# Three small transfers of the softmax denominators moved from SyncE's queue to GpSimd's, with GpSimd held to program order

## The chip, the cores and the metric

The kernel runs on one core of one Trainium2 chip. The metric is the device time of one execution in microseconds (us). The core has five engines that run side by side, each through its own list of instructions in order: TensorE (PE in the profile; its weight loads are PEld), VectorE (DVE), ScalarE (ACT), GpSimd (POOL) and SyncE (SP). SP computes nothing here and issues most of the transfers (DMAs); POOL issues a few of its own. An instruction that waits for a semaphore holds up everything behind it on its engine, and that goes for an issued DMA too.

## What is computed

A layer over 2048 tokens of width 1024: a layer norm, softmax attention with 32 heads of width 32, a gate that routes the best 8 tokens through a SwiGLU network, and their product added to the input.

```python
xn = layernorm(x)
q, k, v = split(xn @ wqkv)                       # 32 heads of 32
o = softmax(q @ k.T / sqrt(32)) @ v              # per head
s = o @ wo
r = xn @ w_r;  idx = top 8 of r over the tokens
y = (silu(xn[idx] @ w_gate) * (xn[idx] @ w_up)) @ w_down * sigmoid(r[idx])
out = x + s * silu(xn with y added at rows idx)
```

## The kernel before

Attention runs over 8 groups g of four heads, 4 blocks qb of 512 queries in each, and 16 key tiles kt in each block: 32 blocks of 16 units. They are numbered here block 0 to 31, and a unit is written (block, kt). In a unit PE makes the scores `sc` of four heads in two halves, ACT takes their exponentials into a tile `pt` of [128, 4 x 512] float32 (L390, two instructions), PE multiplies them with the values into `oa` (L404), and DVE adds `pt` to the block's running sum (`add`, L397, 15 in a block; the first `pt` of a block is itself the sum). PE fills the rest of a unit with the projections of the next groups, in blocks 20 to 28 also with the routed feed-forward network (`ffn` L618, `py` L649). There are five `pt` buffers; one holds the running sum of the block, and for the first units of a block another still holds that of the block before. So an exponential may have to wait for the add of the unit four (early in a block three) before it.

The sum over the 128 partitions of a finished running sum gives the softmax denominators. For blocks 0 to 27 this is done by transfers, called a fold here, numbered like its block. After the end of block b, in units of block b+1:

- unit 1, `fold`: SP stores the sum to DRAM (`a_d`, L438, 1 MB). POOL then issues the ladder, three accumulating DMAs within `a_d` (L440), of 64, 32 and 16 rows added onto as many others, each waiting for the one before.
- unit 9, `fold_load`: the 16 rows left are read back into `dr16` (L446) as 128 x 16 pieces of 16 floats, 64 bytes each.
- unit 12, `fold_rows` and `reciprocals`: DVE sums the 16 rows (L450), takes the reciprocals (L456) and adds to two running checks (L458, L459). One unit later the reciprocals are stored (`r_d`, L462, 128 pieces of 64 bytes), and after that spread over partitions (`rb`, L467, 128 rows of 2 KB).
- units 1 and 2 of block b+2: DVE multiplies the block's output with `rb` (`normalise`, L473), and it is split and stored.

Blocks 28 to 31 (the last group, g == L) get their denominators by matmul (`sums`) and then use the same `reciprocals`.

The order of PE, DVE, ACT and SP is the order in which the program's text issues the work (`manual_schedule`), unit by unit. SP issues in that one order the loads of weights (`wf` L606 and `wd` L611 of the feed-forward network, into three buffers, each waiting for PE to be done with the tile three before; `wo` L691), the stores and loads of q, k and v, and, of each fold, L438, L446, L462 and L467. POOL's order is left to the scheduler of the framework, which issues what is ready first by its own estimate. POOL has few other tasks: two `iota` (L536, L562), a gather of routed rows (L576), a maximum over partitions of weight magnitudes `am` (L1094, `partition_all_reduce`, whose result DVE reads at L1097), and in the last blocks a memset and a gather `up` per tile (L701, L702). Instructions that load another program into POOL stand ahead of the first `iota` and ahead of L1094; order listings show them as `ISA`.

Of the kernel before, what the change touches and what calls it, by code (L numbers as in the profile page):

```python
# [54 lines left out]
@with_exitstack  # L55
def kernel(ctx, tc, x, wqkv, wo, w_r, w_gate, w_up, w_down, out,
                                      general=True, force_general=False):
    nc = tc.nc
    x = x.rearrange("b s d -> (b s) d")
    out = out.rearrange("b s d -> (b s) d")  # L60

    dram = ctx.enter_context(tc.tile_pool(name="dram", bufs=1, space=bass.MemoryType.DRAM))
    keep = ctx.enter_context(tc.tile_pool(name="keep", bufs=1))
    y_d = dram.tile([C, D], F32, name="y_d")
    slot_d = dram.tile([P, NT], I32, name="slot_d")
    ok_i = keep.tile([P, 1], I32, name="ok_i")

    with ExitStack() as st:
        _fast(st, tc, x, wqkv, wo, w_r, w_gate, w_up, w_down, out, dram, y_d, slot_d, ok_i,
              force_general)  # L70

    if general:
        ok = nc.values_load(ok_i[0:1, 0:1], min_val=0, max_val=P)
        with tc.If(ok < P):
            with ExitStack() as st:
                _general(st, tc, x, wqkv, wo, out, dram, y_d, slot_d)
# [28 lines left out]
def _fast(ctx, tc, x, wqkv, wo, w_r, w_gate, w_up, w_down, out, dram, y_d, slot_d, ok_i,  # L105
          force_general):
    nc = tc.nc
# [155 lines left out]
    L = NG - 1  # L263
# [179 lines left out]
    def fold_load(g, qb):  # L443
        a_d = DN[g, qb]
        dr = DN[g, qb] = sb.tile([P, 16, 16], F32, name="dr16", tag="rb", bufs=1)
        nc.sync.dma_start(dr, a_d[0:16].rearrange("r (p q) -> p r q", q=16))  # L446

    def fold_rows(g, qb):
        dr = small.tile([P, 2, 16], F32, name="dr", tag="dr")
        nc.vector.tensor_reduce(dr[:, 0], DN[g, qb].rearrange("p r q -> p q r"), axis=AX.X, op=ALU.add)  # L450
        DN[g, qb] = dr
        return reciprocals(g, qb)

    def reciprocals(g, qb):
        dr = DN[g, qb]
        nc.vector.reciprocal(dr[:, 1], dr[:, 0])  # L456
        r_d = dram.tile([4, 512], F32, name="r_d", tag="r_d", bufs=2)
        nc.vector.tensor_add(den_f, den_f, dr[:, 0])  # L458
        nc.vector.tensor_add(rec_f, rec_f, dr[:, 1])  # L459

        def store():
            nc.sync.dma_start(r_d.rearrange("j (b q) -> (j b) q", q=16), dr[:, 1])  # L462
            return 1, spread

        def spread():
            rb = DN[g, qb] = sb.tile([P, 512], F32, name="rb", tag="rb", bufs=1)
            nc.sync.dma_start(rb, bass.AP(tensor=r_d.tensor, offset=r_d.offset, ap=[[512, 4], [0, 32], [1, 512]]))  # L467

        return 1, store

# [405 lines left out]
    for b in range(NG * NB):  # L876
        g, qb = divmod(b, NB)
        for k, f in (((1, sums), (5, reciprocals), (9, normalise), (10, split_o)) if g == L else
                     ((1, fold), (9, fold_load), (12, fold_rows), (17, normalise), (18, split_o))):
            if b < NG * NB - 1:  # L880
                at((b + 1) * NT + k, f, g, qb)
# [4 lines left out]
    def go(f):  # L886
# [6 lines left out]

    order = ExitStack()
    order.enter_context(tc.manual_schedule(
        engines={mybir.EngineType.PE, mybir.EngineType.DVE, mybir.EngineType.Activation, mybir.EngineType.SP}))


    todo, held, steps = [], [], []
# [98 lines left out]
    for t in range(2, NT + 1):  # L998
# [22 lines left out]
        b, tt = divmod(done, 4)  # L1021
# [27 lines left out]
    for i, u in enumerate(units):  # L1049
        g, qb, kt = u  # L1050
# [27 lines left out]
    for n, f in enumerate(rest_of):  # L1078
        clock[0], ready = len(units) + n, due.pop(len(units) + n, [])
        go(f)  # L1080
        for h in ready + (sides[:1] if n % 2 else []):
            go(h)
        if n % 2:
            sides = sides[1:]
        for k, h in ((2, sums), (12, reciprocals), (24, normalise), (26, split_o)):
            if n == k:
                go(lambda: h(L, NB - 1))
# [172 lines left out]
```

## Time and profile before

| | |
|---|---|
| median of 3 runs | 1640.17 us (1639.65 to 1643.1) |
| profiled execution | 1639.18 us, of which 1637.4 us lie between its first and last instruction |
| busy share of that span | PE 99%, DVE 88%, ACT 72%, POOL 7% |
| granted TensorE clock | 0.998 |
| DMA | 260.87 MB, mean 159 GB/s |

The busy share of PE is an upper mark, since matmuls overlap and their ends are modelled. The span of the profiled execution is what the stretches below add up to; 1.8 us lie outside it.

### The profile page before, as it was taken

Reading aid. Unit: us, or ns where it says so; the run is one execution under the profiler, and the core shown is the slowest. Engines: PE = TensorE matmul, PEld = TensorE weight load, DVE = VectorE, ACT = ScalarE, POOL = GpSimd, SP = SyncE. Lnnn points to the kernel's source line nnn. Section 1 sums busy time; section 2 is a strip of 40 time slices with the busy share of each in tenths; the row PEclk is TensorE's granted clock in tenths of the full one; section 3 lists DMA queues with packets and bytes.
Section 4 is the critical chain, followed back from the end, with each engine's and each line's share of the span. In section 5 each row is a group of like instructions: output and inputs, shape, how many; then the busy total and the mean of one; then the engine's idle time right before and its main releaser. Section 6 shows DMA issues by size and latency. Waiting matters only on the chain.

```text
span 1637.4 us, 59551 instructions
## 1 busy us (share of the span) xinstructions
PE 1615.4 (99%) x27209; PEld 1008.9 (62%) x27209; DVE 1439.4 (88%) x1150; ACT 1178.1 (72%) x1314; POOL 114.8 (7%) x125
## 2 busy tenths in 40 slices
PE   8899999999999999999999999999999999999998
PEld 7646565788875557788655555567454543455566
DVE  8868999999999999999999998888999989787862
ACT  5677777777787787787877877777777777665520
POOL 0000000000000000000000000000000101121010
PEclk9999999999999999999999999999999999999999
DMA  8935555445643454556645577677877877534442
GB/s 286 197 91 131 132 152 139 123 132 131 171 115 83 112 138 116 129 144 163 156 128 145 138 206 198 175 209 213 226 204 211 239 209 206 157 118 139 167 152 94
DMA packets 236093, 260.87 MB, mean 159 GB/s; under 512 B 102994, under 2 KB 183170, under 8 KB 232250
## 3 DMA queue, kind: packets, MB, share of 16 engines
q1 hardware_dynamic: 225866, 231.12, 47.3%
q0 software_dynamic: 9968, 25.87, 10.6%
q8 instruction: 215, 3.52, 0.9%
q14 instruction: 44, 0.36, 0.1%
HBM read 185.25 MB, written 99.43 MB: 174 GB/s over the span
## 4 chain that ended last, share of the span: by engine, by line
PE 83%; DVE 7%; DMA 5%; issue 3%; ACT 1%; SPq 1%; POOL 0%; DVEq 0%; ACTq 0%; POOLq 0%
PE sc L259 23%; PE oa L404 23%; PE proj L259 16%; PE wop L259 10%; PE vp L259 7%; DVE pt L397 3%; DMA a_d<-a_d 2%; PE ffn L618 1%; DMA a_d<-pt 1%; DVE stt L164 1%; PE vp L306 1%; PE py L649 1%; DVE xh L214 1%; ACT pt L390 1%; DMA z<-in_A_x_dram 0%
## 5 line engine op out<-in xcount | busy, mean ns | idle before, releaser
L390 ACT ACTIVATE pt<-sc 128x1024 f32<-128x1024 f32 x1024 | 997.5, 1024 | 343.6 <-PE sc L259 246.5
L397 DVE TENSOR_TENSOR pt<-pt 128x2048 f32<-128x2048 f32 x480 | 1096.1, 2287 | 43.7 <-ACT pt L390 22.1
L259 PE MATMUL sc<-qs,ks 96*32 96x512 f16 x8192 | 658.5, 380 | 3.4 <-ACT pt L390 3.2
L404 PE MATMUL oa<-pt,v 128*32 128x512 f32 x4096 | 551.9, 593 | 0.0
L259 PE MATMUL proj<-xt,w 128*32 128x512 f16 x5664 | 443.5, 379 | 0.0
L259 PEld LDWEIGHTS <-ks 96*32 96x32 f16 x8192 | 293.0, 97 | 119.9 <-issue 19.5
L259 PEld LDWEIGHTS <-w 128*32 128x32 f16 x5664 | 212.5, 96 | 187.0 <-issue 124.6
L404 PEld LDWEIGHTS oa<-pt,v 128*32 128x32 f32 x4096 | 166.0, 110 | 64.4 <-ACT o L415 0.5
L259 PEld LDWEIGHTS <-xt 128*32 128x32 f16 x4608 | 150.4, 96 | 83.8 <-issue 66.6
L259 PE MATMUL vp<-w,xt 128*32 128x256 f16 x4608 | 184.7, 272 | 0.0
L259 PE MATMUL wop<-wo,ot 128*32 128x512 f16 (+1 forms) x3168 | 173.1, 372 | 0.0
L440 POOL DMA_DIRECT2D a_d<-a_d x84 | 67.8, 808 | 1241.2 <-DMA a_d<-pt 939.8
L259 PEld LDWEIGHTS <-ot 128*32 128x32 f16 x3168 | 108.3, 97 | 73.0 <-issue 21.6
L357 DVE SCALAR_TENSOR_TENSOR hl<-proj,hl 128x512 f16<-128x512 f32 x61 | 41.9, 687 | 50.9 <-ACT hl L356 50.8
L763 DVE SCALAR_TENSOR_TENSOR z<-wop,z 128x512 f32<-128x512 f32 (+1 forms) x33 | 22.1, 674 | 59.0 <-PE wop L259 58.8
L306 PE MATMUL vp<-w,xt 128*128 128x256 f16 x384 | 44.1, 273 | 5.1 <-DMA xt<-xh 5.1
L306 PEld LDWEIGHTS <-xt 128*128 128x128 f16 x384 | 36.9, 98 | 11.5 <-DMA xt<-xh 6.6
L618 PEld LDWEIGHTS ffn<-wf,xst 128*32 128x32 f32 x512 | 19.1, 109 | 37.1 <-issue 34.3
L356 ACT ACTIVATE hl<-proj 128x512 f16<-128x512 f32 x61 | 36.4, 596 | 5.1 <-PE proj L259 4.3
L618 PE MATMUL ffn<-wf,xst 128*32 128x224 f32 x512 | 37.3, 352 | 1.1 <-DMA wf<-in_B_w_up_dram 1.1
L249 DVE SCALAR_TENSOR_TENSOR w<-wraw,w 128x1024 f16<-128x1024 f32 x24 | 29.2, 1217 | 3.4 <-ACT w L244 3.3
L252 DVE TENSOR_REDUCE am<-wraw 128x1 f32<-128x1024 f32 x24 | 28.8, 1210 | 0.0
(139 smaller groups left out, 598.2 us busy)
## 6 DMA issues: line engine op xcount, KB each, us to landing
a_d<-pt SPq DMA_DIRECT2D x28, 1024.0 KB
st<-hl SPq DMA_DIRECT2D x64, 256.0 KB
a_d<-a_d POOLq DMA_DIRECT2D x28, 512.0 KB, 6.6
wf<-in_B_w_gate_dram SPq DMA_DIRECT2D x32, 448.0 KB
wf<-in_B_w_up_dram SPq DMA_DIRECT2D x32, 448.0 KB
wd<-in_B_w_down_dram SPq DMA_DIRECT2D x32, 448.0 KB
wraw<-in_A_wqkv_dram SPq DMA_DIRECT2D x24, 512.0 KB
ks<-st SPq DMA_DIRECT2D x96, 128.0 KB
```

What stands on the lines that cost most here:

```text
L249: nc.vector.scalar_tensor_tensor(hl[:, 1], WR[c, g], WS, hl[:, 0], op0=ALU.mult, op1=ALU.subtract)
L252: nc.vector.tensor_reduce(am[:, c * NG + g:c * NG + g + 1], WR.pop((c, g)).rearrange("p k f -> p (k f)"), axis=AX.X, op=ALU.max, apply_abs ...
L259: nc.tensor.matmul(out[c], w[:, c], x, **flags)
L306: nc.tensor.matmul(box["ps"][:, tt], xt[:, xi, k, t % 4 * P:(t % 4 + 1) * P], w[:, :, wi, k, :], start=(n == 0), stop=(n == 23))
L356: nc.scalar.activation(hl[:, 0], ps, AF.Copy, scale=KQ)
L357: nc.vector.scalar_tensor_tensor(hl[:, 1], ps, KQ, hl[:, 0], op0=ALU.mult, op1=ALU.subtract)
L390: nc.scalar.activation(PT[u][:, 2 * hf:2 * hf + 2], ps, AF.Exp, bias=0.0, scale=ESC)
L397: nc.vector.tensor_add(ACC[g, qb], ACC[g, qb], PT[u])
L404: nc.tensor.matmul(OA[g, qb][32 * j:32 * j + 32, :], VT[g, kt // 2][:, kt % 2, 32 * j:32 * j + 32], PT[u][:, j, :], start=(kt == 0), stop= ...
L440: nc.gpsimd.dma_start(a_d[0:n], a_d[n:2 * n], accum_op=ALU.add, max_dma_last_dim=4096)
L618: nc.tensor.matmul(box[i][32 * j:32 * j + 32, :], RT["xst"][:, k, :], wt[:, j * FQ:(j + 1) * FQ], start=(k == 0), stop=(k == KT - 1))
L763: nc.vector.scalar_tensor_tensor(z, box["ps"][:, c0:c0 + width], WOD, z, op0=ALU.mult, op1=ALU.mult)
```

## The change

For blocks 0 to 27 the read of the folded rows (L446), the store of the reciprocals (L462, now L463) and their spread (L467, now L468) are issued by POOL instead of SP. POOL joins the engines that keep program order. For the last group the store and the spread stay on SP. From L456 on, lines after the change are one higher, and from L894 on two higher.

```diff
     def fold_load(g, qb):
         a_d = DN[g, qb]
         dr = DN[g, qb] = sb.tile([P, 16, 16], F32, name="dr16", tag="rb", bufs=1)
-        nc.sync.dma_start(dr, a_d[0:16].rearrange("r (p q) -> p r q", q=16))
+        nc.gpsimd.dma_start(dr, a_d[0:16].rearrange("r (p q) -> p r q", q=16))
...
     def reciprocals(g, qb):
         dr = DN[g, qb]
+        queue = nc.sync if g == L else nc.gpsimd
...
         def store():
-            nc.sync.dma_start(r_d.rearrange("j (b q) -> (j b) q", q=16), dr[:, 1])
+            queue.dma_start(r_d.rearrange("j (b q) -> (j b) q", q=16), dr[:, 1])
             return 1, spread
 
         def spread():
             rb = DN[g, qb] = sb.tile([P, 512], F32, name="rb", tag="rb", bufs=1)
-            nc.sync.dma_start(rb, bass.AP(tensor=r_d.tensor, offset=r_d.offset, ap=[[512, 4], [0, 32], [1, 512]]))
+            queue.dma_start(rb, bass.AP(tensor=r_d.tensor, offset=r_d.offset, ap=[[512, 4], [0, 32], [1, 512]]))
...
     order.enter_context(tc.manual_schedule(
-        engines={mybir.EngineType.PE, mybir.EngineType.DVE, mybir.EngineType.Activation, mybir.EngineType.SP}))
+        engines={mybir.EngineType.PE, mybir.EngineType.DVE, mybir.EngineType.Activation, mybir.EngineType.SP,
+                 mybir.EngineType.Pool}))
```

**SP around fold 27 (block 28).** SP's order before, where the read of the folded rows stands between the loads of `wd`, `wo` and the store and spread of the reciprocals:

```order
L372 DMA qs<-st 32x4x512 x3
L611 DMA wd<-in_B_w_down_dram 112x1024
L446 DMA dr_25496<-a_d 128x16x16
L691 DMA wo_25528<-wo_d 128x1024
L611 DMA wd<-in_B_w_down_dram 112x1024
L691 DMA wo_25528<-wo_d 128x1024
L611 DMA wd<-in_B_w_down_dram 112x1024
L691 DMA wo_25528<-wo_d 128x1024
L462 DMA r_d<-dr 128x16
L691 DMA wo_25528<-wo_d 128x1024
L467 DMA rb<-r_d 128x1x512
```

The same place after the change:

```order
L372 DMA qs<-st 32x4x512 x3
L612 DMA wd<-in_B_w_down_dram 112x1024
L692 DMA wo_25528<-wo_d 128x1024
L612 DMA wd<-in_B_w_down_dram 112x1024
L692 DMA wo_25528<-wo_d 128x1024
L612 DMA wd<-in_B_w_down_dram 112x1024
L692 DMA wo_25528<-wo_d 128x1024 x3
L660 DMA y_d<-y 8x256 x4
```

The three transfers of the fold are gone from SP, and the loads close up. It is the same at every fold.

**POOL around fold 25 (block 26).** POOL's order before: only the ladders, and the maximum `am` between two of them:

```order
L440 DMA a_d<-a_d 128x1024
L440 DMA a_d<-a_d 64x1024
L440 DMA a_d<-a_d 32x1024
L1094 ISA
L1094 ISA am<-am 128x32
L440 DMA a_d<-a_d 128x1024
```

After the change:

```order
L440 DMA a_d<-a_d 64x1024
L440 DMA a_d<-a_d 32x1024
L446 DMA dr_24056<-a_d 128x16x16
L1096 ISA
L1096 ISA am<-am 128x32
L463 DMA r_d<-dr 128x16
L468 DMA rb<-r_d 128x1x512
L440 DMA a_d<-a_d 128x1024
```

The load of POOL's other program and the maximum (now L1096) stand behind the read of fold 25 and ahead of its store and spread. At fold 8 the `iota` L537 with such a load ahead of it stands between the ladder and the read in the same way; before, that load stood at the start of the program, ahead of the other `iota`.

**DVE at fold 25 (block 26).** DVE's order after the change, with the semaphores that each row waits for (DMASW are transfers issued by POOL, Pool is POOL itself):

```order
L397 TENSOR_TENSOR pt<-pt 128x2048 [waits DVE_49,Activation_49]
L450 TENSOR_REDUCE dr<-dr_24056 128x16 [waits DMASW7_49,DMASW2_49]
L1099 TENSOR_REDUCE fl<-am 128x1 [waits Pool_49]
L1100 TENSOR_REDUCE fl<-am 128x1
L457 RECIPROCAL dr<-dr 128x16 [waits DVE_49]
L459 TENSOR_TENSOR den_f<-den_f,dr 128x16
```

Nothing moved on DVE: before, the same rows (L1097 for L1099) stand in the same order. L450 waited for a transfer issued by SP there, and now for POOL's.

## Rows read from the trace of the kernel before

**Rows 1.** The page, parts 1 and 4: busy time of each engine, and the chain of work that ended last by engine.

```profile
PE 1615.4 (99%) x27209; PEld 1008.9 (62%) x27209; DVE 1439.4 (88%) x1150; ACT 1178.1 (72%) x1314; POOL 114.8 (7%) x125
...
PE 83%; DVE 7%; DMA 5%; issue 3%; ACT 1%; SPq 1%; POOL 0%; DVEq 0%; ACTq 0%; POOLq 0%
```

**Rows 2.** Busy time by stretch of 100 us: start and end, length, then PE, PEld, DVE, ACT and POOL busy us (instructions), granted clock, DMA share, GB/s.

```profile
300.00:400.00 100.00, 100.00 (x1803) 80.30 (x1797) 93.66 (x67) 78.22 (x88) 4.81 (x6) 1.00 0.45 121
1300.00:1400.00 100.00, 94.83 (x1402) 41.62 (x1395) 88.68 (x61) 76.00 (x84) 11.35 (x11) 0.98 0.78 212
```

**Rows 3.** Who waited for whom, all engines: us in total, times, longest us.

```profile
PE py L649 <- DMA wd<-in_B_w_down_dram: 1.8, 1, 1.8
...
DVE o L473 <- DMA rb<-r_d: 2.9, 4, 1.0
...
PE ffn L618 <- DMA wf<-in_B_w_up_dram: 1.1, 1, 1.1
```

**Rows 4.** The same for SP's own queue.

```profile
SPq L462 <- DVE rec_f L459: 192.9, 31, 9.7
...
SPq L446 <- DMA a_d<-a_d: 77.7, 24, 6.4
```

**Rows 5.** SP in order of time: start us, us, engine, line, operation, out<-in, count. From folds 0, 25, 26 and 27.

```profile
158.45 0.38 SPq L446 DMA_DIRECT2D dr<-a_d  x1
...
1266.78 0.38 SPq L446 DMA_DIRECT2D dr<-a_d  x1
...
1307.95 0.55 SPq L352 DMA_DIRECT2D v<-v_d  x1
1313.40 0.38 SPq L446 DMA_DIRECT2D dr<-a_d  x1
1313.88 1.50 SPq L606 DMA_DIRECT2D wf<-in_B_w_up_dram  x2
...
1349.17 0.37 SPq L611 DMA_DIRECT2D wd<-in_B_w_down_dram  x1
1355.31 0.38 SPq L446 DMA_DIRECT2D dr<-a_d  x1
...
1357.46 0.43 SPq L611 DMA_DIRECT2D wd<-in_B_w_down_dram  x1
```

**Rows 6.** PE in order of time at folds 26 and 27; in brackets the idle time before a row and what ended it.

```profile
1306.35 0.56 PE L618 MATMUL ffn<-wf,xst 128*32 128x224 f32 x8
...
1318.23 0.59 PE L618 MATMUL ffn<-wf,xst 128*32 128x224 f32 x8 [1.06 <-DMA wf<-in_B_w_up_dram]
...
1351.15 0.62 PE L649 MATMUL py<-wd,ht 112*32 112x256 f32 x8
...
1361.94 1.08 PE L649 MATMUL py<-wd,ht 112*32 112x256 f32 x8 [1.84 <-DMA wd<-in_B_w_down_dram]
```

**Rows 7.** POOL in order of time: the first `iota`, the last ladder step of fold 8, the first and the last step of a ladder (fold 24), and the end of fold 25's ladder with the maximum behind it.

```profile
9.52 0.14 POOL L562 IOTA ti<- 128x16 int32 x1 [9.06 <-issue]
...
503.76 0.78 POOL L440 DMA_DIRECT2D a_d<-a_d  x1 [5.52 <-DMA st<-hl]
...
1207.41 0.83 POOL L440 DMA_DIRECT2D a_d<-a_d  x1 [32.03 <-DMA a_d<-pt]
...
1220.47 0.78 POOL L440 DMA_DIRECT2D a_d<-a_d  x1 [5.12 <-DMA a_d<-a_d]
...
1261.69 0.78 POOL L440 DMA_DIRECT2D a_d<-a_d  x1 [4.40 <-DMA a_d<-a_d]
1270.52 2.38 POOL L1094 PARTITION_ALL_REDUCE am<-am  x1 [8.05 <-DVE am L252]
```

**Rows 8.** The page, part 6: POOL's ladder steps of 128 KB, count, size and median us from issue to landing.

```profile
a_d<-a_d POOLq DMA_DIRECT2D x28, 128.0 KB, 3.5
```

**Rows 9.** Groups of instructions by line on POOL: operation, count, busy us, mean ns of one, idle time before. The gather of 128 rows.

```profile
L702 POOL DMA_INDIRECT up<-y_d,slot_i x16 | 26.6, 1664 | 10.7 <-DMA y_d<-y 6.5 <-POOL up L701 3.5 <-issue 0.6
```

**Rows 10.** DVE in order of time: the first fold's L450, the first use of the `iota` of L536, block 26 around fold 25, and L450 of folds 26 and 27.

```profile
172.27 0.62 DVE L450 TENSOR_REDUCE dr<-dr 128x16 f32<-128x256 f32 x1
...
513.86 0.28 DVE L538 TENSOR_TENSOR hot<-hot,pf 1x128 f32<-1x128 f32 x1
...
1275.03 0.59 DVE L450 TENSOR_REDUCE dr<-dr 128x16 f32<-128x256 f32 x1
1275.54 0.17 DVE L1097 TENSOR_REDUCE fl<-am 128x1 f32<-128x32 f32 x1
...
1276.09 2.28 DVE L397 TENSOR_TENSOR pt<-pt 128x2048 f32<-128x2048 f32 x1
...
1281.29 2.28 DVE L397 TENSOR_TENSOR pt<-pt 128x2048 f32<-128x2048 f32 x1
...
1316.42 0.63 DVE L450 TENSOR_REDUCE dr<-dr 128x16 f32<-128x256 f32 x1
...
1359.52 0.59 DVE L450 TENSOR_REDUCE dr<-dr 128x16 f32<-128x256 f32 x1
```

**Rows 11.** ACT in order of time: the exponentials of units (27, 1) and (27, 3), each unit two instructions, and the first row after a late load in block 29.

```profile
1280.04 1.04 ACT L390 ACTIVATE pt<-sc 128x1024 f32<-128x1024 f32 x1
...
1283.79 1.94 ACT L390 ACTIVATE pt<-sc 128x1024 f32<-128x1024 f32 x2 [0.39 <-PE sc L259]
...
1397.65 1.24 ACT L711 ACTIVATE z<-z,nmr,rstd_r 128x1024 f32<-128x1024 f32 x1 [2.09 <-DMA z<-in_A_x_dram]
```

## The prediction

> **What bounds the kernel now.** The page first: PE is busy for 99% of the span and makes up 83% of the chain that ended last [rows 1]. By stretches, 300 to 400 us shows PE busy for all 100 us and DVE for 93.66: PE sets the pace, and DVE follows with little to spare. From 1300 to 1400 us PE is busy for only 94.83 us [rows 2]. So nearly everywhere this change has nothing to win, and much to lose if it holds up DVE; a gain can come only from the 5 us that PE is idle in blocks 27 to 29. The waits name who causes them: PE waits 1.1 us for a `wf` tile and 1.8 us for a `wd` tile [rows 3].
>
> SP's queue shows why those tiles were late. SP stands at L446 for ladders for 77.7 us in all and at L462 for DVE's reciprocals for 192.9 us [rows 4]. Mostly nobody misses what queues behind. Twice somebody does. At fold 26 SP is done with L352 at 1308.5 us and held at L446 until 1313.40; behind it stands the `wf` load that PE wants at 1317.2 [rows 5, 6]. At fold 27 it is held from 1349.5 to 1355.31, and the `wd` load behind it is issued at 1357.46 for a use that PE reaches at 1360.1 [rows 5, 6].
>
> **What the change removes.** Both holds. The `wf` load needs the buffer of the use at 1306.35, free at 1306.9; without L446 it can go at about 1308.6, 5 us sooner, and PE's idle 1.06 us vanishes. The `wd` load needs the use of 1351.15 to be over, at 1351.8, so it can go at about 1352, also 5 us sooner, and 1.84 us vanish [rows 5, 6]. Sum: -2.9 us. I take it whole, with nothing as the other bound: if the loads are slow for want of bandwidth (DMA share 0.78 there [rows 2]), less is won.
>
> The Trainium skill (DMA: Bandwidth & Descriptors, section "Issuing engines are not separate DMA queues") says that spreading transfers over engines only saves the time an engine's sequencer takes to initiate them, since all run on the same 16 DMA engines. By that rule alone the gain is nothing, since the 0.38 us of an issue is not what held PE, and the sum below would be +3.0 us, 1643.2. The rows show something else to win, the hold of an in-order queue, so I keep the -2.9.
>
> **What it adds on POOL: the price of a transfer.** No plain read or spread by POOL is in the trace; the ladder is nearest. Its first and last steps take 0.83 and 0.78 us to issue, with 128 and 32 rows [rows 7]: 0.5 ns a row on a base of 0.77. The `dr16` read has 2048 pieces, so 0.77 + 2048 x 0.5 = 1.8 us, 1 us more than a ladder step. A ladder step of 128 KB, the read's size, lands 3.5 us after its issue [rows 8]; the read should land after 3.5 + 1.0 = 4.5 us. The low bound is 3.5 (pieces cost nothing). For the high bound the next row is the gather, 1664 ns with 128 rows [rows 9]: (1664 - 770) / 128 = 7.0 ns a row, 14.3 us for 2048, and 17.6 us to landing. I take 4.5, since the ladder is a plain copy of this kind and the gather reads an index per row.
>
> **What waits for the read.** DVE's L450. L446 was issued 11.8 us ahead of L450 in the mean over 28 folds: 13.8 in the first, 3.0 (the least) and 4.2 in the last two [rows 5, 10]. POOL stands ready when the ladder lands, so it issues no later than SP did. With 4.5 us only folds 26 and 27 hold DVE, by 1.5 and 0.3 us. DVE's lateness reaches PE only where an exponential waits for a buffer that a late add frees; the margin there is 1.1 to 1.7 us one block earlier (below). So of fold 26's 1.5 us at most 0.4 gets through, and I charge 0.2, with 0 and 1.5 as bounds; fold 27's 0.3 comes where PE has just won 1.84 us and DVE has less to spare, and I charge it whole.
>
> The store and the spread each start about 0.7 us later than from SP, by the ladder's base, but no longer queue behind SP's loads. `rb` held DVE's L473 four times, 2.9 us in all [rows 3]. I charge nothing; the cover is the two to three units before L473.
>
> **What POOL's order adds.** At fold 25 the load of POOL's other program and the maximum `am` now stand behind the read, and DVE's L1099, which needs the maximum, stands just behind L450 in an order that didn't move. Before, the maximum was over at 1270.52 + 2.38 = 1272.9 us, and DVE asked at 1275.54 [rows 7, 10]. Now: the ladder lands at about 1266.7, when SP issued L446 [rows 5]; POOL issues the read until 1268.5; the program load costs at most the 9.06 us (8.7 without the start's barrier) seen ahead of the first `iota` and at most the 8.05 us seen ahead of the maximum (part of which was the wait for `am`) [rows 7]. I take 8.3: 1276.8. The maximum then ends at 1279.2 at the earliest. With POOL's dispatch and semaphores I say 1279.5, so **DVE stands still for some 3.9 us**.
>
> Who waits for DVE: the add at 1276.09, which ends at 1278.37, frees the buffer that unit (27, 1) writes at 1280.04, a margin of 1.67 us; the add that ends at 1283.57 frees the one for unit (27, 3), written at 1284.7 in the second half of its row, a margin of 1.1 [rows 10, 11]. DVE runs back to back there and can't catch up at once. So ACT is 3.9 - 1.1 = 2.8 us late at the worst, and PE after it; the late load in block 29 shows that PE has next to no slack behind ACT (ACT idle for 2.09 us [rows 11], PE idle for as long). I charge 2.5. The fold's own store and spread come 4 us later too, as late as DVE itself.
>
> At fold 8 the ladder's last issue ends at 504.5; with 8.7 us of program load and 0.3 of `iota` that is 513.5, and DVE wants it at 513.86 [rows 7, 10]. Just hidden: nothing, with 1 us as the other bound.
>
> **The sum.** -2.9 + 2.5 + 0.2 + 0.3 = +0.1 us. The profiled execution took 1639.18 us, so 1639.3; it lies 1.0 us under the median of the runs, so I predict **1640.3 us**, no change that can be told: about 0.2% (3.3 us) is what a measurement of this kernel can tell.
>
> **The rivals.**
> - *Slower, by descriptor generation.* If a piece of 64 bytes costs more than 0.5 ns on POOL, the read is late at folds 24 to 27, and the maximum too. Each further us costs about one at each of folds 25, 26 and 27, so it decides from about 5.6 us to landing (1 ns a piece: 0.1 + 3 x 1.1 = 3.4 us). At 2.5 ns, 8.6 us to landing: -2.9 + 6.6 (fold 25) + 4.5 (fold 26: 5.6 - 1.1) + 4.4 (fold 27: 8.6 - 4.2) = +12.6, 1653. At the gather's 7.0 ns DVE would be held for 5.8 us a fold by the mean lead of 11.8; less the margin of 1.7, times 28, that is 115 us: 1755. For it: nobody has shown 2048 pieces. Against: the ladder's slope is nearly flat. 0.25.
> - *Slower, by POOL and DVE in each other's way.* The Trainium skill (SBUF — State Buffer, the box "The DVE blocks DMA trap (SWDGE)") says that a DMA issued from GpSimd can't get its descriptors written while DVE runs in a 2-port mode. In the rows the ladder's issues keep to 0.78 to 0.83 us beside a DVE that is busy for 88% [rows 1, 7], so this kernel's adds don't block it. Should one add of 2.3 us come in the way of each transfer, the read lands at 6.8 and three waits in a row make L473 late by up to 2 us a fold: some 20 us in all, 1660. 0.07.
> - *Faster.* The program load is shorter or begins while the read is under way, DVE isn't held, and SP, freed, also brings the late load of block 29 forward: -2.9 - 2.1 = -5.0, 1635. For it: 8.05 us is only an upper mark. Against: that load follows the last group's store, which stays on SP. 0.12; -2.9 alone (1637.3) is still within what can't be told.
> - *It doesn't matter.* The holds are passed on to the next wait on SP, and DVE catches up: 1640, within the same bounds. 0.16.
> - The forecast: 0.40.
>
> **How the numbers follow.** Within 0.2%: the forecast, the last rival, and little else: 0.54. Slower: 0.25 + 0.07 and a share of the forecast's own spread, 0.34. Faster: 0.12. The range goes from 1636.5, into the faster case, to 1653, the slow read at 2.5 ns a piece; about 0.08 are left out below and 0.12 above. The forecast's own range is 1638 to 1643.
>
> **What would show it.** Right: PE's two waits for `wf` and `wd` are gone; POOL's issues of L446 last under 2 us; the maximum ends near 1279 us, and DVE shows one idle stretch of about 4 us ahead of L1099 and ACT one of 2 to 3 us soon after; L450 has no wait in most folds. Wrong: issues of L446 that last 5 us or more, or DVE idle ahead of L450 in most folds; no idle ahead of L1099; or PE still waiting for `wd`.

## The result and the profile after

The changed kernel took 1649.85 us in the median of 9 runs (1644.33 to 1657.09), the kernel before 1640.3 us beside it (1637.16 to 1643.1): a ratio of 1.006, with an interval of 1.0044 to 1.0076. It is slower by 0.6%, 9.6 us. The profiled execution after took 1648.64 us, with a span of 1646.8, 9.4 us more than before.

The page after, part 1, busy time of each engine:

```profile
PE 1620.3 (98%) x27209; PEld 1003.0 (61%) x27209; DVE 1438.9 (87%) x1150; ACT 1178.6 (72%) x1314; POOL 185.1 (11%) x209
```

Beside [rows 1] this row already splits the loss in two. The span grew by 9.4 us, and PE was busy for 4.9 us more with the same 27209 matmuls; so 4.5 us are new idle time, and 4.9 us are the same work done more slowly. DVE and ACT did the same work in the same time.

Who waited for whom after, all engines (us in total, times, longest us):

```profile
DVE dr L450 <- DMA dr<-a_d: 12.5, 4, 5.3
...
ACT pt L390 <- DVE pt L397: 12.4, 12, 4.3
PE sc L259 <- ACT pt L390: 12.1, 9, 3.5
DVE o L474 <- DMA rb<-r_d: 8.4, 4, 4.9
...
ACT z L712 <- DMA z<-in_A_x_dram: 3.6, 1, 3.6
...
DVE fl L1099 <- POOL am L1096: 2.6, 1, 2.6
...
PE py L650 <- DMA wd<-in_B_w_down_dram: 0.3, 1, 0.3
```

PE's waits for `wf` and `wd` [rows 3] are gone but for 0.3 us. In their place DVE waits for the read of the folded rows (L450) and for the maximum (L1099), and PE waits for exponentials, which wait for DVE's adds (12.4 us; 6.2 us before). The wait for the spread (L473, now L474) grew from 2.9 to 8.4 us.

Fold 25 in order of time, POOL and then DVE, ACT and PE (start us, us; in brackets the idle time before and what ended it):

```profile
1268.65 0.79 POOL L440 DMA_DIRECT2D a_d<-a_d  x1 [6.78 <-DMA a_d<-a_d]
1273.76 1.23 POOL L446 DMA_DIRECT2D dr<-a_d  x1 [4.32 <-DVE y L656]
1282.64 0.45 POOL L1096 PARTITION_ALL_REDUCE am<-am  x1 [7.66 <-issue]
1283.87 0.74 POOL L463 DMA_DIRECT2D r_d<-dr  x1 [0.78 <-DVE rec_f L460]
```

```profile
1279.89 0.60 DVE L450 TENSOR_REDUCE dr<-dr 128x16 f32<-128x256 f32 x1 [4.00 <-DMA dr<-a_d]
1283.13 0.19 DVE L1099 TENSOR_REDUCE fl<-am 128x1 f32<-128x32 f32 x1 [2.64 <-POOL am L1096]
```

```profile
1286.07 1.94 ACT L390 ACTIVATE pt<-sc 128x1024 f32<-128x1024 f32 x2 [3.74 <-DVE fl L1104]
```

```profile
1287.15 0.61 PE L259 MATMUL sc<-qs,ks 96*32 96x512 f16 x8 [3.07 <-ACT pt L390]
```

DVE stands still twice, 4.00 us for the read and 2.64 us for the maximum, and 3.07 us of that arrive at PE. The 7.66 us ahead of the maximum are put down to the load of POOL's other program, which stands there in POOL's order and has no row of its own; the profile names nothing else that ends this idle time.

Fold 27, the same, without a maximum in the way:

```profile
1355.67 0.78 POOL L440 DMA_DIRECT2D a_d<-a_d  x1 [6.42 <-DMA a_d<-a_d]
1362.68 1.24 POOL L446 DMA_DIRECT2D dr<-a_d  x1 [6.23 <-DMA a_d<-a_d]
```

```profile
1369.31 0.58 DVE L450 TENSOR_REDUCE dr<-dr 128x16 f32<-128x256 f32 x1 [5.28 <-DMA dr<-a_d]
```

```profile
1373.76 0.80 PE L259 MATMUL sc<-qs,ks 96*32 96x512 f16 x8 [3.54 <-ACT pt L390]
```

From the ladder's last issue to the read's it takes 7.0 us, and the data are there 6.6 us after the read's issue. Before, the last step was issued here, 4.6 us ahead of SP's read at 1355.31 [rows 5]:

```profile
1350.76 0.78 POOL L440 DMA_DIRECT2D a_d<-a_d  x1 [6.63 <-DMA a_d<-a_d]
```

Fold 24, where the sum of the prediction had no wait, after (POOL, then DVE); before, the last step was issued at 1220.47 [rows 7] and SP's read at 1223.77:

```profile
1223.68 0.79 POOL L440 DMA_DIRECT2D a_d<-a_d  x1 [4.88 <-DMA a_d<-a_d]
1229.62 1.23 POOL L446 DMA_DIRECT2D dr<-a_d  x1 [5.14 <-DMA a_d<-a_d]
...
1233.92 0.60 DVE L450 TENSOR_REDUCE dr<-dr 128x16 f32<-128x256 f32 x1 [3.10 <-DMA dr<-a_d]
```

DVE is ready for L450 at its start less its wait. How long before that moment the read was issued, and what it took to land, in us (fold 25's landing is not on record; its 6.1 is the time to L450's start):

| fold | issued ahead of DVE, before | issued ahead of DVE, after | issue to landing, after | L450 waits, after |
|---|---|---|---|---|
| 24 | 6.9 | 1.2 | 4.2 | 3.1 |
| 25 | 8.3 | 2.1 | 6.1 | 4.0 |
| 26 | 3.0 | 7.1 | 7.3 | 0.15 |
| 27 | 4.2 | 1.4 | 6.5 | 5.3 |

So two things make the read late. At folds 24, 25 and 27 it is issued 3 to 6 us later beside DVE, mostly because the ladder ahead of it ends later; and at folds 25 to 27 it lands slowly. At fold 24 the ladder's last step goes out 3.2 us later and lands after 5.3 us, before after 3.2; SP's `wf` load, which stood behind the read at 1224.24 before, now goes at 1221.67, ahead of that step. Had it landed after 4.5 us everywhere, DVE would still wait for 3.3, 2.4 and 3.1 us at folds 24, 25 and 27.

Next the stretches behind PE's three large gaps (columns as in [rows 2]); the last gap is the one behind the late `z` load of block 29. PE at that load, after and then before:

```profile
1408.50 1.96 PE L259 MATMUL sc<-qs,ks 96*32 96x512 f16 x16 [3.51 <-ACT pt L390]
```

```profile
1400.37 0.62 PE L259 MATMUL sc<-qs,ks 96*32 96x512 f16 x8 [2.03 <-ACT pt L390]
```

The stretches after:

```profile
1288.70:1292.10 3.40, 3.40 (x32) 1.35 (x28) 3.40 (x3) 1.91 (x3) 0.00 (x0) 0.50 0.51 172
...
1374.10:1377.50 3.40, 3.40 (x32) 1.10 (x24) 3.30 (x3) 2.57 (x3) 0.33 (x1) 0.50 0.24 78
...
1408.20:1411.60 3.40, 3.10 (x24) 1.03 (x27) 3.40 (x4) 3.40 (x5) 0.00 (x0) 0.50 0.01 4
```

Behind each gap TensorE runs for 3.4 us at a granted clock of 0.50, the 1.2 GHz level, and does 1.7 us of work in that time. This is the second half of the loss. Before, there was one such stretch in this part of the program, behind the wait for `wd`; behind the gap at the `z` load there was none:

```profile
1361.90:1365.30 3.40, 3.36 (x28) 1.25 (x32) 3.20 (x2) 1.39 (x2) 0.95 (x1) 0.50 0.87 238
...
1400.50:1404.00 3.50, 3.20 (x52) 1.45 (x48) 3.50 (x4) 3.50 (x5) 0.00 (x0) 1.00 0.02 5
```

So the change's account is: waits for `wf` and `wd` -2.6 us; gaps at folds 24, 25 and 27 of 0.6, 3.07 and 3.54; the gap at the `z` load +1.5; two more stretches of half clock, +3.4. That is +9.5 us; differences in the first 100 us, one further stretch of half clock among them, nearly cancel.

### The profile page after: what moved, and what is told of

It reads as the page before. It is cut to its first block, busy times and chain, and to the rows that moved or that the text cites. A ratio compares the mean times of both kernels' runs of the same rounds, so it can differ in the third digit from the quotient of the medians.

```text
span 1646.8 us, 59540 instructions
## 1 busy us (share of the span) xinstructions
PE 1620.3 (98%) x27209; PEld 1003.0 (61%) x27209; DVE 1438.9 (87%) x1150; ACT 1178.6 (72%) x1314; POOL 185.1 (11%) x209
## 4 chain that ended last, share of the span: by engine, by line
PE 79%; DVE 9%; DMA 8%; issue 2%; ACT 1%; SPq 0%; DVEq 0%; POOL 0%; ACTq 0%; POOLq 0%
PE sc L259 22%; PE oa L404 21%; PE proj L259 15%; PE wop L259 10%; PE vp L259 7%; DVE pt L397 6%; DMA a_d<-a_d 2%; DMA a_d<-pt 1%; DMA dr<-a_d 1%; PE vp L306 1%; PE ffn L619 1%; DMA xt<-xh 1%; ACT pt L390 1%; PE projw L283 1%; DMA r_d<-dr 1%
## 5 line engine op out<-in xcount | busy, mean ns | idle before, releaser
L259 PE MATMUL sc<-qs,ks 96*32 96x512 f16 x8192 | 673.1, 380 | 12.1 <-ACT pt L390 12.1
L404 PE MATMUL oa<-pt,v 128*32 128x512 f32 x4096 | 560.6, 595 | 0.0
L259 PE MATMUL proj<-xt,w 128*32 128x512 f16 x5664 | 453.1, 379 | 0.0
L259 PEld LDWEIGHTS <-ks 96*32 96x32 f16 x8192 | 297.0, 97 | 139.8 <-issue 29.8
L259 PE MATMUL vp<-w,xt 128*32 128x256 f16 x4608 | 189.2, 272 | 0.0
L259 PEld LDWEIGHTS <-ot 128*32 128x32 f16 x3168 | 117.1, 97 | 64.9 <-issue 21.0
L463 POOL DMA_DIRECT2D r_d<-dr x28 | 16.5, 588 | 308.0 <-DVE rec_f L460 308.0
L446 POOL DMA_DIRECT2D dr<-a_d x28 | 34.6, 1235 | 113.2 <-DMA a_d<-a_d 57.7
```

The lines of the kernel that those rows point to most:

```text
L259: nc.tensor.matmul(out[c], w[:, c], x, **flags)
L404: nc.tensor.matmul(OA[g, qb][32 * j:32 * j + 32, :], VT[g, kt // 2][:, kt % 2, 32 * j:32 * j + 32], PT[u][:, j, :], start=(kt == 0), stop= ...
L446: nc.gpsimd.dma_start(dr, a_d[0:16].rearrange("r (p q) -> p r q", q=16))
L463: queue.dma_start(r_d.rearrange("j (b q) -> (j b) q", q=16), dr[:, 1])
```

## The experiments

Three theories stood after the result. **A**: at fold 25 the program load and the maximum behind the read make the loss. **B**: a read that POOL issues is slow, because POOL issues it. **C**: the loads that SP can now issue sooner share the DMA engines with the ladder and the read. Each run is set against runs of the kernel before on the same chip; runs on different chips are compared by their ratios. The times are medians, the traces single executions.

**POOL in program order, nothing else.**

```diff
-        engines={mybir.EngineType.PE, mybir.EngineType.DVE, mybir.EngineType.Activation, mybir.EngineType.SP}))
+        engines={mybir.EngineType.PE, mybir.EngineType.DVE, mybir.EngineType.Activation, mybir.EngineType.SP,
+                 mybir.EngineType.Pool}))
```

> The kernel before with only one part of the change: GpSimd joins the engines held to program order, and all transfers stay on SP. Theory A (the program load and the maximum behind fold 25's read make the loss), theory B (a read issued by POOL starts later behind the ladder and lands later, so that DVE is held at folds 24, 25 and 27) and theory C (the loads that SP can now issue sooner share the DMA engines with the ladder and the read) all expect no change here, 1640 us within 2: there is no read or store on POOL for the maximum to stand between, the maximum should end near 1273 us, and PE's waits for wf (1.1) and wd (1.8) stay. Only if holding POOL to program order costs by itself would it come to 1644 or more.

Measured: 1639.44 us, ratio 1.0003 (0.9995 to 1.0012); the waits for `wf` and `wd` were 1.0 and 2.0 us. The order by itself costs nothing while the transfers stay on SP.

**The maximum out of fold 25's way.**

```diff
+    def am_max():
+        nc.gpsimd.partition_all_reduce(am, am, channels=P, reduce_op=RED.max)
+        return 8, am_rows
...
+    on(L, 0, 15, am_max)
...
     order.close()
...
-    nc.gpsimd.partition_all_reduce(am, am, channels=P, reduce_op=RED.max)
```

(`am_rows` holds DVE's two reductions; unit (L, 0, 15) is the last of block 28.)

> The changed kernel with the maximum am and its two DVE reductions issued behind fold 27's spread instead of between fold 25's read and store. Theory A: the whole of fold 25's loss goes, PE's gap of 3.07 us at 1284 and the 1.7 us of half clock behind it, so 1649.9 - 4.8 = 1645. Theories B and C: DVE's wait of 4.0 us for the read at fold 25 stays, 2.3 to 2.9 us of it past the margin of 1.1 to 1.7 us; the gap shrinks to some 2 us, and 1 to 3 us are won: 1647 to 1649. In all three fold 27 stays as it is: L450 waits 5.3 us, PE idle 3.5, half clock behind it.

Measured: 1648.56 us, ratio 1.0049 (1.0035 to 1.0063), against 1.006 (1.0044 to 1.0076) of the changed kernel: 1.3 us less by the medians, 1.8 us by the ratios, within what the two intervals leave open. Waits in its trace:

```profile
DVE dr L450 <- DMA dr<-a_d: 12.7, 4, 6.7
...
PE sc L259 <- ACT pt L390: 9.5, 7, 4.0
```

L450 waits as long as in the changed kernel (12.5 us), now mostly at fold 24 (6.7 us), and PE's gaps at folds 24 to 27 add up to 7.3 us, where they were 7.2. So A is at most a small part; the read is late with or without it, and at which of the last folds it hurts changes from one execution to another.

**The read back on SP, store and spread on POOL** (and the maximum late).

```diff
-        nc.gpsimd.dma_start(dr, a_d[0:16].rearrange("r (p q) -> p r q", q=16))
+        nc.sync.dma_start(dr, a_d[0:16].rearrange("r (p q) -> p r q", q=16))
```

> x3_max_late with the read of the folded rows back on SP; the store and the spread stay on POOL. Theory A: no gain over x3_max_late, 1645, and PE's waits for wf and wd return on top. Theories B and C: DVE is held ahead of L450 at no fold, the gaps of 3 us at folds 25 and 27 and the half clock behind them are gone, PE's waits for wf (1.1) and wd (1.8) are back: 1640 to 1641. If store and spread on POOL cost by themselves, L474 waits for rb for more than the 8.4 us of the changed kernel and the time stays above 1643.

Measured: 1642.22 us, ratio 1.0014 (1.0005 to 1.0023), 6.3 us under the run before. No wait of DVE for the read is left in its trace, and the waits for `wf` and `wd` are back (1.4 and 2.3 us). So the read carries most of the loss: 6.3 of the 8.9 us that the run before lay above its kernel before. About 2 us stay (0.8 to 3.8 by the interval), which only the moved store and spread (or the moved maximum) can hold; DVE waits 6.0 us for `rb`, before 2.9.

**SP held for the ladder as before, the read on POOL** (and the maximum late).

```diff
         nc.gpsimd.dma_start(dr, a_d[0:16].rearrange("r (p q) -> p r q", q=16))
+        gate = small.tile([1, 16], F32, name="gate16", tag="gate16")
+        nc.sync.dma_start(gate, a_d[0:1, 0:16])
```

> x3_max_late with one transfer of 64 bytes added on SP at the place where L446 stood: it reads 16 numbers of the folded sum into a tile that nobody uses, and so holds SP for the ladder as before. Theory B (the read is slow because POOL issues it): the read lands as late as in the changed kernel, 5.7 to 6.3 us after its issue at folds 25 to 27, L450 waits 3 to 5 us at folds 24, 25 and 27, and PE's waits for wf and wd come on top: 1648 to 1652. Theory C (the freed loads slow ladder and read): the read lands 3.3 to 4 us after its issue at these folds, L450's waits are gone or under 1.5 us: 1640 to 1643.

Measured: 1652.95 us, ratio 1.0085 (1.0067 to 1.0103). It is the slowest so far, as B said, but the reason isn't B's. DMA issues from 1200 to 1400 us, folds 24 to 27 (KB each, median us from issue to landing): the ladder's last step and the read, first of the changed kernel, then of this one. Of four ladder steps, and of the reads of the changed kernel, three landings each are on record.

```profile
a_d<-a_d POOLq DMA_DIRECT2D x4, 128.0 KB, 5.3
dr<-a_d POOLq DMA_DIRECT2D x4, 128.0 KB, 6.5
```

```profile
a_d<-a_d POOLq DMA_DIRECT2D x4, 128.0 KB, 3.3
dr<-a_d POOLq DMA_DIRECT2D x4, 128.0 KB, 8.8
```

With SP held the ladder's last step is as fast as before (3.3 in the same stretch of the kernel before), and the read is slower than in the changed kernel. SP in its trace shows why: the gate transfer goes when the ladder has landed, and the loads pile in behind it, while POOL issues the read at 1363.23.

```profile
1362.78 0.23 SPq L448 DMA_DIRECT2D gate<-a_d  x1
1363.06 0.34 SPq L694 DMA_DIRECT2D wo<-wo_d  x1
1363.45 0.56 SPq L614 DMA_DIRECT2D wd<-in_B_w_down_dram  x1
1364.05 0.43 SPq L694 DMA_DIRECT2D wo<-wo_d  x1
1364.60 0.36 SPq L614 DMA_DIRECT2D wd<-in_B_w_down_dram  x1
```

It suggests a C of another form: what counts is which loads run beside the ladder and the read. The run with the loads held until the read has landed, below, tests it.

**L450 and what follows two units later at folds 24 to 27, normalise one** (and the maximum late).

```diff
             if b < NG * NB - 1:
+                k += {fold_rows: 2, normalise: 1, split_o: 1}.get(f, 0) if 24 <= b < 28 else 0
                 at((b + 1) * NT + k, f, g, qb)
```

> x3_max_late with the users of the read moved later at folds 24 to 27 only: DVE's L450 and all behind it two units later, normalise and split one unit later. All transfers of the folds stay on POOL. If DVE's wait for the late read is the price: L450's waits of 3 to 7 us are gone, with them PE's gaps (0.6, 3.1 and 3.5 us in the changed kernel) and the half clock behind the two large ones (1.7 us each), so 1649.9 - 7.2 - 3.4 = 1639.3; the gap behind block 29's z load (3.5 us) and its half clock stay. If it is the store and the spread, or the traffic on the DMA engines, that costs: L474's waits for rb grow and the time stays at 1645 or more.

Measured: 1649.16 us, ratio 1.0066 (1.005 to 1.0082): no gain, but by a fault of this kernel. L450's waits fell to 1.4 us, and no gap over 0.7 us is left at folds 24 to 26. At fold 27 the later store now came ahead of the maximum, and the spread behind it:

```profile
1369.29 0.59 POOL L463 DMA_DIRECT2D r_d<-dr  x1 [6.99 <-DVE rec_f L460]
1375.85 1.18 POOL L866 PARTITION_ALL_REDUCE am<-am  x1 [5.97 <-DMA wo<-wo_d]
1376.90 0.89 POOL L468 DMA_DIRECT2D rb<-r_d  x1
```

```profile
1389.06 1.04 PE L259 MATMUL sc<-qs,ks 96*32 96x512 f16 x8 [8.35 <-ACT pt L390]
```

The maximum, with 5.97 us of idle time ahead of it that fits the program load, stands between store and spread; DVE waits 10.0 us for `rb`, and PE has a gap of 8.35 us, with 10.2 us of half clock from 1384.3 us on. That is theory A's mechanism after all, at a place where it costs: a program load of POOL in the chain of a fold.

**The same with the `z` loads of block 29 two units earlier.**

```diff
-            at(nxt + ((7, 2, 1)[qb] + 4 * tt if qb < NB - 1 else (-2, -1, 1, 2)[tt]), gate_load, qb, tt)
+            at(nxt + ((5, 2, 1)[qb] + 4 * tt if qb < NB - 1 else (-2, -1, 1, 2)[tt]), gate_load, qb, tt)
```

> x6_rows_late with the loads z of block 29 issued two units earlier, ahead of the last group's store and spread on SP. If the gap of 3.5 us at 1405 is the z load held in SP's queue, it goes, and the half clock behind it: 3.5 + 1.7 = 5.2 us less than x6_rows_late, 1634. If the gap is something else that only ends there, no more than 1 us is won.

Measured: 1646.72 us, ratio 1.0053 (1.0034 to 1.0072), 2.4 us under the run before. It has the fault of the run before, with a gap of 8.29 us, and says little of `z`.

**The kernel before with the same edit of the `z` loads, and nothing else.**

> The kernel before with the z loads of block 29 two units earlier and nothing else: PE's gap of 2.03 us at 1398 goes, no half clock stood behind it: 1640.0 - 2.0 = 1638. The waits for wf (1.06) and wd (1.85) stay, and the half clock of 3.4 us behind the latter.

Measured: 1635.72 us, ratio 0.9987 (0.9979 to 0.9996), 2.5 us under its kernel before. ACT's wait for `z` and PE's gap of 2.03 us are gone. Its profiled execution also has a shorter wait for `wd`, 0.5 us, with no half clock behind it, which the edit doesn't explain. This is the lowest ratio of the study, by an edit of one number, though only 0.13% under the kernel before.

**SP alone, with the read one unit later at folds 26 and 27.** It was meant to put the read behind the `wf` and `wd` loads. With `z` early as above.

```diff
+                k += {fold_load: 1, fold_rows: 2, normalise: 1, split_o: 1}.get(f, 0) if 26 <= b < 28 else 0
```

> The kernel before, all transfers on SP, with the read at folds 26 and 27 one unit later (so behind the wf and wd loads in SP's order), their L450 two units later, normalise and split one unit later, and the z loads of block 29 two units earlier. If SP's hold is all that the change can win, this wins it without POOL: 1640.0 - 1.06 - 1.85 - 2.03 and the half clock behind the wd wait, 1.7: 1633.4. If the loads pass the wait on to the next transfer on SP, or the read now lands late behind them: 1637 or more.

Measured: 1638.72 us, ratio 1.0001 (0.9991 to 1.001), so 3 us over the run before. At fold 26 a `wf` load now goes ahead of the read, at 1308.40, and the wait for `wf` is gone. At fold 27 the edit misses its aim: the `wd` load that PE waits for still stands behind the read on SP.

```profile
1355.66 0.38 SPq L446 DMA_DIRECT2D dr<-a_d  x1
1356.08 1.02 SPq L611 DMA_DIRECT2D wd<-in_B_w_down_dram  x1
```

So PE's wait for `wd`, 1.4 us with half clock behind it, is left, and this run doesn't say what that hold is worth. The later spread makes DVE wait for `rb` (3.4 us at the longest).

**The fault of `x6_rows_late` mended.** The maximum stands behind fold 27's spread, and normalise and split are two units later.

```diff
-    on(L, 0, 15, am_max)
+    on(L, 1, 0, am_max)
...
-                k += {fold_rows: 2, normalise: 1, split_o: 1}.get(f, 0) if 24 <= b < 28 else 0
+                k += {fold_rows: 2, normalise: 2, split_o: 2}.get(f, 0) if 24 <= b < 28 else 0
```

> x6_rows_late mended: the maximum stood between the store and the spread of fold 27 there, and now stands behind the spread (one unit later); normalise and split of folds 24 to 27 are two units later instead of one. If DVE's wait for what POOL's transfers bring late is the price: PE's gaps at folds 24, 25 and 27 are gone with their half clock, 7 us and 3.4 us, 1639 to 1640; only the gap behind the z load (3.5 us) and its half clock are left of the loss. If the crowded DMA engines or the clock cost without a wait of DVE, it stays at 1645 or more.

Measured: 1640.74 us, ratio 1.001 (1.0 to 1.0021). The read's landing takes as long as in the changed kernel:

```profile
dr<-a_d POOLq DMA_DIRECT2D x4, 128.0 KB, 6.5
```

but L450 stands far enough behind it (1.2 us of waiting in all), no gap of PE over 0.8 us is left at folds 24 to 27 and no half clock, and with them 8 of the 9.6 us are gone. DVE's wait for the late data was the price, not the traffic. The gap behind `z`, 4.2 us here with 6.8 us of half clock, is left.

**The same with `z` early.**

> x10_rows_later with the z loads of block 29 two units earlier. If nothing else of the change costs, the rest of the loss goes too, and SP's freed loads are a gain: 3 to 5 us less than x10_rows_later, 1634 to 1636, no slower than x8_before_z (1635.7). If POOL's store and spread cost by themselves, as the 1642.2 of x4_read_sp hints: 1637 to 1639.

Measured: 1637.15 us, ratio 0.9993 (0.9984 to 1.0002); 3.6 us less, as expected, but in the range of the other branch, a price of store and spread by themselves. It isn't faster than the kernel before with `z` early alone (0.9987): nothing is seen of what SP's freedom should have brought. PE waits for `wd` twice here, 2.7 us in all; whether store and spread cost too stays open, since the two intervals overlap.

**The loads held until the read has landed** (`x5_sp_held`, but the 64 bytes come from `dr16`).

```diff
-        nc.sync.dma_start(gate, a_d[0:1, 0:16])
+        nc.sync.dma_start(gate, dr[0:1, 0, :])
```

> x5_sp_held with the 64-byte transfer on SP reading from dr16 instead of from the folded sum, so that SP's loads start only when POOL's read has landed. If the reads of x5_sp_held landed late (7.4 to 9.5 us after their issue at folds 24, 25 and 27) because the loads started in the moment when the ladder was done, the read now lands as in the quiet folds, 3.3 to 4 us after its issue, and L450's waits at folds 24 to 27 shrink from 17 us to some 4; PE's waits for wf and wd grow by the 5 us that the loads lose: 1645 to 1652. If a read from POOL is slow in these folds by itself, it lands after 5.5 us and more as before, L450 waits for 12 us and more, and the time is above 1655.

Measured: 1655.54 us, ratio 1.0107 (1.0093 to 1.0121). By the time alone this would be B's branch (above 1655); the trace decides for the other. From 1200 to 1400 us:

```profile
a_d<-a_d POOLq DMA_DIRECT2D x4, 128.0 KB, 3.6
dr<-a_d POOLq DMA_DIRECT2D x4, 128.0 KB, 4.1
```

```profile
PE ffn L621 <- DMA wf<-in_B_w_up_dram: 8.8, 2, 5.3
...
DVE dr L452 <- DMA dr<-a_d: 1.9, 1, 1.9
```

With SP's loads held back a read that POOL issues lands after 4.1 us in the same folds, where it took 6.5 and 8.8 us. L450 (L452 here) waits once, 1.9 us. B falls: POOL is not what makes the read slow. What does is the company of SP's loads. The other half of it is in the kernel before: at fold 26 SP issued the read at 1313.40 and two `wf` loads right behind it, from 1313.88 on [rows 5], and DVE used the data at 1316.42 [rows 10], 3.0 us after the issue; from POOL, beside the loads, the same fold's read took 7.3 us. The price of keeping the loads away is paid by PE, which waits 8.8 us for `wf` and 3.3 us for `wd`; that is more than was expected (1645 to 1652).

**The read of folds 26 and 27 alone on POOL**, these two folds' L450, normalise and split two units later, `z` early, POOL not in program order.

```diff
-        nc.sync.dma_start(dr, a_d[0:16].rearrange("r (p q) -> p r q", q=16))
+        (nc.gpsimd if 4 * g + qb in (26, 27) else nc.sync).dma_start(
+            dr, a_d[0:16].rearrange("r (p q) -> p r q", q=16))
...
+                k += {fold_rows: 2, normalise: 2, split_o: 2}.get(f, 0) if 26 <= b < 28 else 0
```

> x8_before_z with the read of folds 26 and 27 alone issued by POOL, with L450, normalise and split of these two folds two units later; POOL is not held to program order, store and spread stay on SP. If the hold of SP is a real price and the late read is covered by the two units: PE's waits for wf (1.2) and wd (0.5 to 1.9) go, 1635.7 - 1.7 = 1634 and never above 1636. If the later store and spread hold SP or DVE instead, 1636 to 1639.

Measured: 1638.69 us, ratio 0.9997 (0.9987 to 1.0006), 0.4 us under its kernel before, where `z` alone was 2.5 us under its own; the intervals overlap. It is not the 1634 expected of a real price of the hold. The wait for `wf` is gone, and so is the one at the `wd` tile that the read held up before (used at 1360.82 here). But PE waits at the tiles before and behind it:

```profile
1356.42 0.64 PE L650 MATMUL py<-wd,ht 112*32 112x256 f32 x8 [1.24 <-DMA wd<-in_B_w_down_dram]
1360.82 0.62 PE L650 MATMUL py<-wd,ht 112*32 112x256 f32 x8
1364.86 0.64 PE L650 MATMUL py<-wd,ht 112*32 112x256 f32 x8 [1.70 <-DMA wd<-in_B_w_down_dram]
```

In the kernel before, the DMA engines are full around that place, with a DMA share of 1.00 and 290 GB/s:

```profile
1358.00:1361.90 3.90, 1.79 (x24) 0.40 (x16) 3.86 (x6) 2.40 (x3) 0.00 (x0) 1.00 1.00 290
```

The load of the last of these tiles goes 4.7 us sooner (1353.71 on SP, before 1358.46) and still lands only at 1364.9; before, PE used that tile at 1365.75 without a wait. So what one tile gains its neighbours lose; that the full engines are the reason is likely, but no run separates it. The trace also has a gap of PE of 2.19 us at 1399.65, with 3.4 us of half clock behind it, where DVE waits 3.7 us for the last group's `rb` (2.0 us and no gap with `z` alone), so not all of the difference lies in the two folds.

## Why the prediction was right or wrong

The forecast was no change, 1640.3 us. The time lay 9.6 us above it, with an interval that leaves no change out, so the forecast itself failed; the stated range (to 1653) holds the time. That is luck in part: its upper end was the rival of slow descriptors, 2.5 ns a piece, and a piece costs 0.2 ns of POOL's time. The step that failed is the one on who waits for the read: at folds 24, 25 and 27 POOL issues it later than was taken, and at folds 25 and 27 it lands later too. Step by step:

- **The holds vanish (-2.9).** Right for this trace: -2.6 us. The runs with the read off SP at folds 26 and 27 and its users moved (`x10_rows_later`, `x11_later_z`, `x13_two_folds`) show `wf` won each time, and the one `wd` wait that was named won too, with others at its neighbours (0.6, 2.7 and 2.9 us of waits). The bound "less is won, for want of bandwidth" was the better value for the `wd` term.
- **The price of the read.** The issue was put at 1.8 us and is 1.24 in the mean of 28; the landing was put at 4.5 us and is 4.2 in the median of all folds. Both good, and yet the step failed at the folds where it mattered: at fold 24 the landing takes 4.2 us, but at folds 25 to 27 some 6.1, 7.3 and 6.5. The 3.5 us for a ladder step [rows 8] was a median over 28 folds, used for four in which the DMA share is 0.78 instead of 0.45 [rows 2]. The change also brings SP's loads forward to the ladder and the read; the prediction saw that they can go 5 us sooner, and did not ask what they would run beside.
- **"POOL issues no later than SP did."** Wrong, and the larger part: the lead over DVE shrank from 6.9, 8.3 and 4.2 us to 1.2, 2.1 and 1.4 at folds 24, 25 and 27. At fold 27 the read is issued 2.5 us later behind the last ladder step, about 2 us of it because the step itself lands later (6.4 against 4.4 us); the medians of the step from 1200 to 1400 us are 5.3 and 3.3. With SP held for the ladder (`x5_sp_held`) the step is back at 3.3.
- **Folds 26 and 27 (+0.2 and +0.3).** L450's waits were put at 1.5 and 0.3 us and were 0.15 and 5.28. Folds 24 and 25, where no wait for the read was forecast, waited 3.1 and 4.0 us. The rival with a slow read comes nearest: by its own rule, 6.5 us to landing give 0.1 + 3 x 2.0 = +6.1 us. But its cause is wrong, since descriptors are not slow, and it has no later issue.
- **Fold 25 (+2.5).** The hold behind the read is there as said: a program load of 7.7 us (8.3 said), the maximum at its end, DVE idle ahead of L1099 and PE 3.07 us late. But the maximum ended at 1283.1 instead of 1279.5, since the read itself was issued 7 us later than assumed, and the run with the maximum moved away has as long gaps at folds 24 to 27 (7.3 us against 7.2) with no maximum there.
- **Store and spread (0).** Mis-sized: 8.4 us of waits at L474, some 2 us of time (0.8 to 3.8), by the run with the read back on SP, which holds the moved maximum too.
- **Fold 8 (0).** Right: the `iota` was over at 511.84, and DVE used it at 513.69 without a wait.
- **The clock.** Missing from the sum: +3.4 us. The row with the `wd` wait at 1360.1 stood there [rows 6], and the stretch behind it, at 0.50, was not looked at; the 0.98 of the granted clock from 1300 to 1400 [rows 2] said that it was there. The two new gaps of 3.07 and 3.54 us cost 1.7 us more each by the half clock behind them.
- **The `z` load.** The faster rival had it come sooner with SP freed. It came later behind the same last group's spread (3.55 us of ACT's idle time, 2.09 before), and moving it is the only edit here that won time beyond its interval (2.5 us, `x8_before_z`).

On the rule cited from the Trainium skill ("DMA: Bandwidth & Descriptors", "Issuing engines are not separate DMA queues"): the runs agree with it in the sum. The read of POOL suffers from the loads of SP (6.5 and 8.8 us beside them, 4.1 without), and in the end moving the issue won nothing that a run shows. The end of the hold, which took away the 1.06 us for `wf`, is something that the rule doesn't speak of. Another section of that page of the Trainium skill, "Queues, rings and completion order", says that each DMA engine serves the queue rows in turn, a packet at a time. That fits what is seen: on SP's own queue the read stood ahead of the loads (3.0 us at fold 26), and on POOL's it has to share with them (7.3). The runs don't show the turns themselves. Of the trap that the Trainium skill describes in "SBUF — State Buffer", the box "The DVE blocks DMA trap (SWDGE)", no run shows a sign: L446's 28 issues take 1235 ns in the mean beside a DVE that is busy for 87%.

## What to carry to other kernels

A transfer that stood in one queue ahead of others came first here; moved to another queue, it freed the ones behind it and had to share with them. Before such a move, look at what runs beside the transfer in the stretch where its landing matters, and take the landing time from that stretch, not from a median over the program. Where the last transfer of a chain gets later, move its users later too: two units here took back 8 of 9.6 us. Count a gap of the matrix engine with the half clock behind it. And look at where an edit of the order has put the instructions: `x9_before_shift` moved one load past the read and left the other behind it.

## What the runs showed of the hardware that was not expected

- A read with 2048 pieces of 64 bytes takes POOL 1.24 us to issue, against 0.38 us on SP and 0.78 to 0.83 us for a ladder step [rows 5, 7]: 0.2 ns a piece over the ladder's issue, less than half of the estimate. It lands after 4.1 us without other loads beside it.
- Gaps of PE and the half clock behind them (granted clock 0.50): 1.84 us and 3.4 (before, at `wd`), 3.07 us and 3.4, 3.54 us and 3.4 (after), 8.35 us and 10.2 (`x6_rows_late`); 2.19 us and 3.4 (`x13_two_folds`, behind the last group's `rb`). The gap of 2.03 us behind `z` before had none, nor had one of 2.74 us there in `x1_order`. So the length of the gap alone doesn't tell.
- A load of POOL's other program has no row of its own in the trace. It shows as idle time of POOL in which nothing is issued: 7.66 us ahead of the maximum in the changed kernel, with "issue" as its end, and 5.97 to 7.88 us there in the runs with the maximum moved, mostly put down to some transfer that ended then.
